# Tokens' values loaded behind the turn of P, with a fourth buffer of turned inputs, in a two-layer recurrent-memory attention kernel

## Chip, cores and metric

One core of one Trainium2 chip runs the whole program. The metric is the device time of one execution in microseconds, from runs without a profiler; the profile is one further execution with its own time.

## What is computed

Four sub-layers follow each other on x (2048 tokens, 512 features): attention with a recurrent memory (A), a dense layer with relu (B), A again, B again, each on the normalized input and added to x. A cuts the tokens into 64 segments of 32; each is preceded by 8 memory rows, which are the first 8 output rows of the segment before, so the segments of one A must run in order. 32 heads of 128. Cut from the reference:

```python
for s in range(n_seg):
    h = jnp.concatenate([mem, xs], axis=1)            # 8 + 32 rows
    q, k, v = (jnp.einsum('btd,dhe->bhte', h, W) for W in (Wq, Wk, Wv))
    scores = jnp.einsum('bhqe,bhke->bhqk', q, k) * scale
    p = softmax(jnp.where(mask, scores, -1e9))
    o = jnp.einsum('bhqk,bhke->bhqe', p, v)
    o = jnp.einsum('bhte,hed->btd', o, Wo)
    mem = o[:, :M, :]
    outs.append(o[:, M:, :])
...
x = x + A(layernorm(x)); x = x + relu(layernorm(x) @ w1) @ w2
x = x + A(layernorm(x)); x = x + relu(layernorm(x) @ w1) @ w2
```

## The kernel before

**Steps.** The program is written out as 68 steps, k = 0 to 67. Step k runs segment k of the first A (layer a = 0, k up to 63) and segment k - 4 of the second A (layer a = 1, k from 4), side by side: layer 0 on rows 0 to 39 of the tiles, layer 1 on rows 64 to 103. Steps 0 to 3 and 64 to 67 have one layer (`single`), steps 4 to 63 two. The dense layer of what ended two steps ago (`dense_h`, `dense_y`) and the output projection of the step before (`output_x`, tiles `wox`) run between as filler. TensorE, VectorE (DVE), SyncE (SP) and GpSimd (POOL) execute in the order in which the program is written; only ScalarE's (ACT) order is left to the scheduler.

**One two-layer step**, as `step` (L895) writes it: queries and keys of heads 0 to 15 (`qk`, L575); the value rows of this step's tokens are loaded from DRAM into `Vs` (`load_values`, called at L911); the normalized rows of earlier segments are turned by a DMA transpose (`transpose_step`, L289, tile `xnT`); the value rows of the memory are loaded (`load_memory_values`, L775); scores of these heads; then, behind the first batch of the queries of heads 16 to 31, `probabilities` (L926): softmax, whose last product into `P_sb` is POOL's (L646), and `turn_p` (L663), one DMA transpose of P into `PT0`, and in steps with k%4 = 3 `inputs_T`, a DMA transpose of 128 tokens of x. Dense and output filler; scores and softmax of the second half; `dense_y`; the second half of P is turned on TensorE (`transpose_p`, L656) and copied by ACT and DVE (L660); `weighted_v` (L682) multiplies P by `Vs`; `output_mem` (L617) and `new_memory` make the next memory: ACT copies `wm` (L814), TensorE turns it (`mt`, L820), and its values (`memory_values`, L765) are computed and stored to DRAM (L770).

**Values of tokens.** Layer 1's values are computed one step ahead (`values1`, L346) and stored to DRAM (`vd1`, L351). Layer 0's are, for k%4 < 2, a by-product of `memory_values` (DRAM tiles `vmd`); for the other two segments of each four they are computed in groups by `values0(p, n)` (L306): pair of segments p, and n of 0, 2, 4, 6, each 8 matmuls of 128x512, one ACT copy to a `vst` tile (L312) and one store to `vd0[p]` (L313). `load_values` therefore issues two DMAs (L742) for layer 0 and one (L737) for layer 1 when k%4 < 2, and one for each (L746, L737) otherwise. `values_at(k)` says which groups step k computes and `block` where they lie in it. In two-layer steps these are steps with k%4 = 1, where `output_x` has nothing to do. Before the change: step 1 three groups, step 5 two, steps 9 to 37 three each, steps 41 to 61 four each. `split(k)` (two or three groups) also splits `dense_h` around the second scores; with four groups it stays whole.

**Inputs.** x is handled 128 tokens at a time: `load_xb` (SP), `moments_x` (DVE, one `pow` on POOL), `normalize` (DVE, L227), `inputs_T` into `xT0[n]`. Step k handles n = k//4 + 3: load at k%4 = 0, moments at k%4 = 1, normalize at the end of k%4 = 2, transpose at k%4 = 3. `xT0` has three buffers; at step 1 a copy of n = 3 is turned on TensorE into the buffer of `ob`.

**SP's queue.** All DMAs but the loads of residual rows (POOL) and two at the end are issued by SP in program order; a DMA that waits for its data holds up all behind it.

Of the kernel before, what the change touches and what calls it, by code (L numbers as in the profile page):

```python
# [7 lines left out]
BF = mybir.dt.bfloat16  # L8
F32 = mybir.dt.float32
# [13 lines left out]
def kernel(  # L23
# [191 lines left out]
    xT0, xnT_tiles, hT_tiles, vd0, vd1, vmds, wm_tiles, wo_tiles, xp_tiles, vp_tiles, obs = {}, {}, {}, {}, {}, {}, {}, {}, {}, {}, {}  # L215

    def stat_tail(stats, of=""):
        mv = wk.tile([128, 2], F32, tag="ln_mv" + of, bufs=2 - len(of), name="mv")
        nc.vector.bn_aggr(out=mv[:], in_=stats[:])
        rstd = wk.tile([128, 1], F32, tag="ln_rstd" + of, bufs=2 - len(of), name="rstd")  # L220
        nc.vector.tensor_scalar_add(out=rstd[:], in0=mv[:, 1:2], scalar1=LN_EPS)
        nc.gpsimd.tensor_tensor(out=rstd[:], in0=rstd[:], in1=mhalf_t[:], op=ALU.pow)
        return mv, rstd

    def normalize(eng, dst, src, mom, lo, hi):
# [12 lines left out]
            nc.tensor.transpose(tp[:, c4, :], xn[:, c4 * 128:(c4 + 1) * 128], ident[:])  # L238
        return tp

    def inputs_T(n, early=False):
        tag, bufs = ("ob", 1) if early else ("xT0", 3)
        xT0[n] = wk.tile([128, NC4, 128], BF, tag=tag, bufs=bufs, name="xT0")
        if n < 3 or early:
            tp = transpose_pe(xbs[n])
            nc.scalar.copy(out=xT0[n][:], in_=tp[:])
        else:
            nc.sync.dma_start_transpose(out=xT0[n][:], in_=xbs[n][:])
# [47 lines left out]
    def values0(p, n, lo=0, hi=NC4, pool=None, stage=None):  # L296
        r = 64 * (p % 2)
        if (n, lo) == (0, 0):
            vd0[p] = dram.tile([4, 2, 64, 512], BF, tag="vd0", bufs=3, name="vd0")
        if lo == 0:  # L300
            pool, tag = (pool, "wo") if pool else (ps_fill, "fill")
            vp_tiles[p, n] = pool.tile([128, 512], F32, tag=tag, name="vp")
        vp = vp_tiles[p, n]
        for c4 in range(lo, hi):
            for j in range(2):
                nc.tensor.matmul(vp[64 * j:64 * j + 64, :], lhsT=xT0[p // 2][:, c4, r:r + 64],  # L306
                                 rhs=Wv_sb[:, c4, (n + j) * 512:(n + j + 1) * 512],
                                 start=(c4 == 0), stop=(c4 == NC4 - 1), tile_position=(0, 64 * j))
        if hi < NC4:
            return  # L310
        vst = wk.tile([128, 512], BF, tag="vst", bufs=5, name="vst")[:] if stage is None else stage
        nc.scalar.copy(out=vst, in_=vp[:])  # L312
        nc.sync.dma_start(out=vd0[p][n // 2].rearrange("j t e -> (j t) e"), in_=vst)  # L313
# [95 lines left out]
    def last_rows(k, eng):  # L409


        r = 64 * (LAST - k)
        R = residual(LAST - 1)
        if not last_t:
            last_t["stats"] = wk.tile([128, 2, 6], F32, tag="ln_last", bufs=1, name="stats")
            last_t["mv"] = wk.tile([128, 2], F32, tag="ln_mvl", bufs=1, name="mv")
            last_t["rstd"] = wk.tile([128, 1], F32, tag="ln_rstdl", bufs=1, name="rstd")
        stats, mv, rstd = (last_t[x][r:r + 64] for x in ("stats", "mv", "rstd"))
        nc.vector.bn_stats(out=stats[:, 0, :], in_=R[r:r + 64, 0:256])
        for j in range(2):  # L420
            nc.vector.tensor_copy(out=last_t["stats"][r + 32 * j:r + 32 * j + 32, 1, :],
                                  in_=last_t["stats"][r + 32 - 32 * j:r + 64 - 32 * j, 0, :])
        nc.vector.bn_aggr(out=mv, in_=stats.rearrange("p n s -> p (n s)"))
        nc.vector.tensor_scalar_add(out=rstd, in0=mv[:, 1:2], scalar1=LN_EPS)
        nc.gpsimd.tensor_tensor(out=rstd, in0=rstd, in1=mhalf_t[r:r + 64, :], op=ALU.pow)
        eng.tensor_scalar(out=XN[r:r + 64, 0:256], in0=R[r:r + 64, 0:256], scalar1=mv[:, 0:1], scalar2=rstd[:, 0:1],
                          op0=ALU.subtract, op1=ALU.mult)
# [234 lines left out]
    def turn_p():  # L662
        nc.sync.dma_start_transpose(out=PT0[:], in_=P_sb[:].rearrange("p s k -> p (s k)"))  # L663
# [116 lines left out]
    def block(k, lo, hi):  # L780
        output_x(k - 1, lo, hi)
        groups = values_at(k)
        if split(k):

            rest = [(i, 0, NC4) for i in range(1, len(groups))]
            if k == 1:
                todo = [] if lo == 0 else [(0, 0, 2)] if hi == 16 else [(0, 2, NC4)] + rest
            else:
                todo = [(0, 0, 2)] if lo == 0 else [(0, 2, NC4)] if hi == 16 else rest
        else:  # L790
            todo = [(i, c4, c4 + 2) for i in range(len(groups)) for c4 in range(0, NC4, 2)
                    if lo < 8 * i + 2 * c4 + 2 <= hi]
        for i, c_lo, c_hi in todo:
            p, n = groups[i]
            values0(p, n, c_lo, c_hi, ps_wo if i in (0, 3 if len(groups) == 4 else 2) else None)

    def split(k):
        return len(values_at(k)) in (2, 3)
# [1 line left out]
    def values_at(k):  # L800


        if k in (1, 5):
            return [(5, 6), (7, 0), (7, 2)] if k == 1 else [(7, 4), (7, 6)]
        if k % 4 != 1 or not has0(k + 1):
            return []
        groups = [(p, n) for p in range(9, NSEG // 2, 2) for n in range(0, NCH, 2)]
        i = k // 4 - 2
        lo = 3 * min(i, 8) + 4 * max(i - 8, 0)
        return groups[lo:lo + (3 if i < 8 else 4)]  # L810

    def new_memory(k, cont, wo):
        wm_sb = wm_tiles[k] = wk.tile([128, Dm], BF, tag="vst", bufs=5, name="wm")
        nc.scalar.copy(out=wm_sb[:], in_=wo[:])  # L814
        values1(k + 1, 0)
        c = 1 - k % 2
        mt = ps_c.tile([128, NC4, 2, M], F32, tag="c", name="mt")
        for c4 in range(NC4):
            for r in range(0, 128, 32):
                nc.tensor.matmul(mt[r:r + 32, c4].rearrange("p a m -> p (a m)"),  # L820
                                 lhsT=wm_sb[:, c4 * 128 + r:c4 * 128 + r + 32],
                                 rhs=sel[:, 4 * M * c:4 * M * c + 2 * M], start=True, stop=True,
                                 tile_position=(0, r))
        lo, hi = cont[0], cont[-1] + 1

        single = len(layers(k)) == 1
        by_act = k == 0 or has1(k + 1)

        def to_values():
            copy = nc.scalar.copy if by_act else nc.vector.tensor_copy  # L830
            copy(out=HTm[:, :, lo * M:hi * M], in_=mt[:, :, lo:hi, :].rearrange("p c a m -> p c (a m)"))

        def to_queries():
            nc.vector.tensor_copy(out=HT[:, :, lo:hi, 0:M], in_=mt[:, :, lo:hi, :])  # L834

        for f in (to_values, to_queries) if single else (to_queries, to_values):
            f()
# [57 lines left out]
    def step(k):  # L895
        act = layers(k)
        single = len(act) == 1
        cont = [a for a in act if k - DELTA * a + 1 < NSEG]
        n_x = k // 4 + 3
        has_x = n_x < NXT  # L900
        by_pe = k in (1, LAST)
        ahead = has1(k + 1) or not cont
        if k % 4 == 0 and has_x:
            load_xb(n_x)
        with tc.high_priority(offset=PRIO):
            behind = norm_rows.pop(k, None)
            if k == 1:
                def behind():
                    normalize(nc.vector, xbs[n_x], xbs[n_x], moments_x(n_x), 0, 128)
            qks = qk(0, act, behind=behind)  # L910
            load_values(k, act)  # L911
            if k == 1:
                memory_values(k)
                inputs_T(n_x, True)
        part = 4 if k == LAST else 8 if single else 5
        mid = 8 if k == LAST else 16

# [8 lines left out]
        def probabilities():  # L926

            softmax(0, act, by_pe, ess)
            if not by_pe:
                turn_p()  # L930
            if k % 4 == 3 and has_x:
                inputs_T(n_x)
            if has0(k + 1):
                load_x(k + 1)
            if k == 1:
                load_dense()
# [27 lines left out]
            add_output(k - 1)  # L964
        if k == LAST:
            add_last(k - 1, 0)
        if k % 4 == 1 and k > 1 and has_x:
            mom["x"] = moments_x(n_x)
        with tc.high_priority(offset=PRIO):
            transpose_p(1)  # L970
# [38 lines left out]
                memory_values(k + 1)  # L1009
        with tc.high_priority(offset=PRIO):  # L1010
            prepare(k + 1)
        if k % 4 == 2 and k > 2 and has_x:
            normalize(nc.vector, xbs[n_x], xbs[n_x], mom["x"], 0, 128)

    mom = {}
    with tc.manual_schedule(engines={mybir.EngineType.PE, mybir.EngineType.DVE, mybir.EngineType.SP,
                                   mybir.EngineType.Pool}):
        load_rest()
        mem0T = const.tile([128, NC4, M], BF)
        tp = transpose_pe(mem0)  # L1020
        nc.vector.tensor_copy(out=mem0T[:], in_=tp[:, :, 0:M])
        for a in range(2):
            nc.vector.tensor_copy(out=HT[:, :, a, 0:M], in_=mem0T[:])
            nc.vector.tensor_copy(out=HTm[:, :, a * M:(a + 1) * M], in_=mem0T[:])
        for n in range(2):
            m = moments_x(n)
            normalize(nc.vector, xbs[n], xbs[n], m, 0, 128)
# [74 lines left out]
```

## Time and profile before

| | us |
|---|---|
| three runs | 1595.73, 1600.38, 1601.42; median 1600.38 |
| the profiled execution | 1596.61 |
| its span, first to last instruction | 1594.8 |
| busy in it: PE / weight loads / DVE / ACT / POOL | 1565.9 / 1320.7 / 1268.4 / 738.9 / 349.8 |

The page names a group of instructions by line, engine, operation and tiles, with its count, busy time and mean duration. These are the groups that the change touches:

| group | count | busy us | mean ns |
|---|---|---|---|
| PE L306, value groups of layer 0 | 512 | 64.5 | 383 |
| PE L682, P times values | 4096 | - | 176 |
| ACT L312, copy of a group's values | 53 (+11 into weight tiles) | 30.6 | 582 |
| DVE L232, moments of x | 16 | 11.0 | 686 |
| DVE L227, normalize of x | 16 | 6.4 | 400 |

Matmuls overlap in the pipeline, so the mean duration of one says less than the time from the first of a run of them to the first of the next. An SP line shows only the issue of a DMA; when its data moves is seen in the trace's DMA packets, which carry a start, a size and a queue.

### The profile page before, as it was taken

To read this page: it belongs to the slowest core of one execution; us is meant where nothing else is said; L and a number is where in the kernel's file an instruction comes from. 1 tells how busy PE (TensorE), PEld (TensorE's weight loads), DVE (VectorE), ACT (ScalarE), POOL (GpSimd) and SP (SyncE) were. 2 spreads that over 40 slices of the span, in tenths; PEclk is the share of its full clock that TensorE was granted. 3 is DMA by queue.
4 is the path that set the end of the run, shared out by engine and by line. 5 is a ranking of instruction groups with operands and counts; after the bars stand their busy time and mean duration, and the time that the engine had idled before them with its cause. 6 is when DMAs were issued, how large, how long until landed. Compare 5 with 4: busy or idle time off the path is not lost.

```text
span 1594.8 us, 94682 instructions
## 1 busy us (share of the span) xinstructions
PE 1565.9 (98%) x42680; PEld 1320.7 (83%) x42680; DVE 1268.4 (80%) x3115; ACT 738.9 (46%) x1799; POOL 349.8 (22%) x670
## 2 busy tenths in 40 slices
PE   6999999999999999999999999999999999999998
PEld 4677888888898888889888888988888898898886
DVE  4578888888888888888888888888878888887866
ACT  3434444444544544454454545445454544545433
POOL 2012222222222222222222222222222222222110
PEclk9999999999999999999999999999999999999999
DMA  9733343343343534444334443343443333233332
GB/s 369 237 78 74 76 87 89 65 98 86 77 78 83 94 64 95 84 73 87 83 87 71 98 83 77 84 83 82 80 98 79 74 88 79 78 77 93 70 75 41
DMA packets 222564, 146.38 MB, mean 92 GB/s; under 512 B 124008, under 2 KB 216528, under 8 KB 222160
## 3 DMA queue, kind: packets, MB, share of 16 engines
q1 hardware_dynamic: 218992, 136.09, 37.6%
q8 instruction: 335, 5.49, 1.5%
q0 software_dynamic: 3072, 4.20, 1.1%
q14 instruction: 69, 0.57, 0.1%
q10 hardware_dynamic: 96, 0.03, 0.0%
HBM read 65.41 MB, written 45.35 MB: 69 GB/s over the span
## 4 chain that ended last, share of the span: by engine, by line
PE 96%; DMA 2%; DVE 1%; SPq 1%; issue 0%; ACT 0%; POOL 0%; POOLq 0%; ACTq 0%
PE qp L575 38%; PE wox L365 10%; PE wo L617 8%; PE vm L765 7%; PE v L346 7%; PE hp L507 6%; PE sp L528 5%; PE pv L682 4%; PE sp L609 4%; PE vp L306 3%; DMA Wv_sb<-in_A_Wv_dram 2%; PE tp L656 1%; PE xp L478 1%; PE wox L388 1%; SPq L134 0%; PE mt L820 0%
## 5 line engine op out<-in xcount | busy, mean ns | idle before, releaser
L581 ACT CAST QT<-qp 128x480 bf16<-128x480 f32 (+3 forms) x408 | 201.7, 494 | 392.3 <-PE qp L575 392.2
L575 PE MATMUL qp<-HT,Wq_sb 128*128 128x80 bf16 (+1 forms) x8704 | 370.2, 200 | 2.1 <-POOL HT L754 1.2
L575 PE MATMUL qp<-HT,Wk_sb 128*128 128x80 bf16 (+1 forms) x8704 | 369.2, 199 | 1.5 <-DMA Wk_sb<-in_A_Wk_dram 0.7
L575 PEld LDWEIGHTS <-Wq_sb 128*128 128x128 bf16 x8704 | 325.6, 100 | 33.8 <-issue 26.5
L575 PEld LDWEIGHTS <-Wk_sb 128*128 128x128 bf16 x8704 | 328.2, 100 | 2.3 <-DMA Wk_sb<-in_A_Wk_dram 1.2
L583 DVE CAST KT<-qp 128x480 bf16<-128x480 f32 (+3 forms) x408 | 231.4, 568 | 124.0 <-PE qp L575 118.1
L646 POOL TENSOR_TENSOR P_sb<-es,sm 128x320 bf16<-128x320 f32 x185 | 130.9, 721 | 751.7 <-ACT es L631 502.2
L365 PE MATMUL wox<-Wo_sb,OTx 128*64 128x256 bf16 x2880 | 173.6, 273 | 0.0
L625 DVE TENSOR_REDUCE mx<-sp 128x8 f32<-128x320 f32 x256 | 115.0, 487 | 73.6 <-PE sp L609 72.7
L365 PEld LDWEIGHTS <-OTx 128*64 128x64 bf16 x2880 | 150.2, 110 | 2.9
L631 ACT ACTIVATE es<-es 128x320 f32<-128x320 f32 x256 | 110.7, 469 | 58.2 <-DVE es L629 57.2
L765 PE MATMUL vm<-Wv_sb,HTm 128*32 128x512 bf16 x2176 | 136.4, 380 | 0.6 <-DVE HT L834 0.6
L641 DVE TENSOR_REDUCE sm<-es 128x8 f32<-128x320 f32 x256 | 118.3, 462 | 15.0 <-ACT es L631 4.7
L617 PE MATMUL wo<-Wo_sb,OTm 128*32 128x512 bf16 x2144 | 128.9, 380 | 0.2 <-issue 0.2
L346 PE MATMUL v<-Wv_sb,xnT 128*32 128x512 bf16 x2048 | 129.0, 378 | 0.0
L601 DVE CAST sp<-maskb 128x320 f32<-128x320 bf16 x256 | 118.4, 484 | 0.0
L629 DVE TENSOR_TENSOR es<-sp,mx 128x320 f32<-128x320 f32 x256 | 113.8, 483 | 1.5
L765 PEld LDWEIGHTS <-HTm 128*32 128x32 bf16 x2176 | 90.6, 96 | 27.4 <-issue 12.3
L528 PE MATMUL sp<-w_sb,hT 128*64 128x256 bf16 (+4 forms) x1452 | 104.1, 275 | 0.2 <-issue 0.2
L769 ACT CAST VmS<-vm 128x512 bf16<-128x512 f32 x134 | 78.6, 587 | 53.8 <-PE vm L765 53.8
L507 PE MATMUL hp<-xnT,w_sb 128*128 128x64 bf16 (+3 forms) x2948 | 102.2, 193 | 0.5 <-DVE xnT L436 0.4
L507 PEld LDWEIGHTS <-w_sb 128*128 128x128 bf16 (+1 forms) x2948 | 95.1, 101 | 1.3 <-issue 0.7
(124 smaller groups left out, 2028.8 us busy)
## 6 DMA issues: line engine op xcount, KB each, us to landing
Vs<-vd SPq DMA_DIRECT2D x96, 256.0 KB
vd<-vst SPq DMA_DIRECT2D x181, 128.0 KB
vmd<-VmS SPq DMA_DIRECT2D x134, 128.0 KB
Vs<-vmd SPq DMA_DIRECT2D x254, 32.0 KB
Vs<-vmd SPq DMA_DIRECT2D x60, 128.0 KB
Wq_sb<-in_A_Wq_dram SPq DMA_DIRECT2D x2, 2048.0 KB
Wk_sb<-in_A_Wk_dram SPq DMA_DIRECT2D x2, 2048.0 KB
Wv_sb<-in_A_Wv_dram SPq DMA_DIRECT2D x2, 2048.0 KB
```

The costliest lines, as they stand in the source:

```text
L346: nc.tensor.matmul(vp[32 * j:32 * j + 32, :], lhsT=tokens[:, c4, :], rhs=Wv_sb[:, c4, n * 512:(n + 1) * 512], start=(c4 == 0), stop=(c4 == ...
L365: nc.tensor.matmul(out[64 * j:64 * j + nr, 0:256], lhsT=lhsT, rhs=rhs[:, 256 * j:256 * j + 256], start=start, stop=stop, tile_position=(0, ...
L507: nc.tensor.matmul(hp[0:fs, fc - f0, 0:n], lhsT=w1_sb[:, c4, fc * 128:fc * 128 + fs], rhs=cols(c4), start=(c4 == 0), stop=(c4 == NC4 - 1))
L528: nc.tensor.matmul(sp_banks[bank][64 * j:64 * j + n, 0:w], lhsT=hT_tiles[d][0:fs, fc, 0:n], rhs=w2_flat[0:fs, fc * Dm + 256 * j:fc * Dm + ...
L575: nc.tensor.matmul(qp[:, hi, 0:ncol], lhsT=W_sb[:, c4, h * Dh:(h + 1) * Dh], rhs=HT[:, c4, a_lo:a_hi, :], start=(c4 == 0), stop=(c4 == NC4 ...
L581: nc.scalar.copy(out=dst[:, 0:nh, a_lo * L:a_hi * L], in_=qp[:, 0:nh, 0:ncol])
L583: nc.vector.tensor_copy(out=dst[:, 0:nh, a_lo * L:a_hi * L], in_=qp[:, 0:nh, 0:ncol])
L601: nc.vector.tensor_copy(out=sp_tiles[a], in_=maskb2)
L617: nc.tensor.matmul(wo[32 * j:32 * j + 32, :], lhsT=OTm[:, h, n, 2 * M * c:2 * M * c + 4 * M], rhs=Wo_sb[:, h, :], start=(h < 4), stop=(h > ...
L641: nc.vector.tensor_reduce(out=sm[:], in_=es[:], axis=AX.X, op=ALU.add)
L646: eng.tensor_tensor(out=P, in0=es[:], in1=sm[:].unsqueeze(2).to_broadcast([128, 8, L]), op=ALU.mult)
L765: nc.tensor.matmul(vp[32 * j:32 * j + 32, :], lhsT=HTm[:, c4, :], rhs=Wv_sb[:, c4, n * 512:(n + 1) * 512], start=(c4 == 0), stop=(c4 == NC ...
```

## The change

Three things are done. The groups of `values_at` are dealt out anew: (7, 4) goes to step 2, inside `new_memory`, between the copy of `wm` and the matmuls on it; (7, 6) to step 4, in the second part of `block`; the groups of pairs from 9 on begin at step 5 in place of step 9, three to a step up to step 49 and four in steps 53, 57 and 61. x is handled four steps earlier (n = k//4 + 4, beginning with a load, moments and normalize in step 2), `xT0` and `vd0` have four buffers, and the early copy in the buffer of `ob` is gone. In two-layer steps `load_values` is called in `probabilities`, behind `turn_p`, and no longer before `transpose_step`. Mean, variance and inverse deviation share a tile, the last rows' moments use a slot of `es`, and `mem0T` is gone: the turned memory is copied from PSUM four times.

```diff
     def stat_tail(stats, of=""):
-        mv = wk.tile([128, 2], F32, tag="ln_mv" + of, bufs=2 - len(of), name="mv")
-        nc.vector.bn_aggr(out=mv[:], in_=stats[:])
-        rstd = wk.tile([128, 1], F32, tag="ln_rstd" + of, bufs=2 - len(of), name="rstd")
+        mom = wk.tile([128, 3], F32, tag="ln_mv" + of, bufs=2 - len(of), name="mv")
+        mv, rstd = mom[:, 0:2], mom[:, 2:3]
+        nc.vector.bn_aggr(out=mv, in_=stats[:])
...
-    def inputs_T(n, early=False):
-        tag, bufs = ("ob", 1) if early else ("xT0", 3)
-        xT0[n] = wk.tile([128, NC4, 128], BF, tag=tag, bufs=bufs, name="xT0")
-        if n < 3 or early:
+    def inputs_T(n):
+        xT0[n] = wk.tile([128, NC4, 128], BF, tag="xT0", bufs=4, name="xT0")
+        if n < 4:
...
-            vd0[p] = dram.tile([4, 2, 64, 512], BF, tag="vd0", bufs=3, name="vd0")
+            vd0[p] = dram.tile([4, 2, 64, 512], BF, tag="vd0", bufs=4, name="vd0")
...
+        elif k < 5:
+            todo = [(0, 0, NC4)] if k == 4 and lo else []
...
     def values_at(k):
-        if k in (1, 5):
-            return [(5, 6), (7, 0), (7, 2)] if k == 1 else [(7, 4), (7, 6)]
+        if k < 5:
+            return {1: [(5, 6), (7, 0), (7, 2)], 2: [(7, 4)], 4: [(7, 6)]}.get(k, [])
...
-        i = k // 4 - 2
-        lo = 3 * min(i, 8) + 4 * max(i - 8, 0)
-        return groups[lo:lo + (3 if i < 8 else 4)]
+        i = k // 4 - 1
+        lo = 3 * min(i, 12) + 4 * max(i - 12, 0)
+        return groups[lo:lo + (3 if i < 12 else 4)]
...
         values1(k + 1, 0)
+        if k == 2:
+            values0(*values_at(k)[0])
         c = 1 - k % 2
...
-        n_x = k // 4 + 3
+        n_x = k // 4 + 4
...
-        if k % 4 == 0 and has_x:
+        if (k % 4 == 0 or k == 2) and has_x:
             load_xb(n_x)
...
             qks = qk(0, act, behind=behind)
-            load_values(k, act)
+            if single:
+                load_values(k, act)
...
             if not by_pe:
                 turn_p()
+            if not single:
+                load_values(k, act)
             if k % 4 == 3 and has_x:
                 inputs_T(n_x)
...
-        if k % 4 == 1 and k > 1 and has_x:
+        if (k % 4 == 1 and k > 1 or k == 2) and has_x:
             mom["x"] = moments_x(n_x)
...
-        if k % 4 == 2 and k > 2 and has_x:
+        if k % 4 == 2 and has_x:
             normalize(nc.vector, xbs[n_x], xbs[n_x], mom["x"], 0, 128)
...
-        mem0T = const.tile([128, NC4, M], BF)
         tp = transpose_pe(mem0)
-        nc.vector.tensor_copy(out=mem0T[:], in_=tp[:, :, 0:M])
         for a in range(2):
-            nc.vector.tensor_copy(out=HT[:, :, a, 0:M], in_=mem0T[:])
-            nc.vector.tensor_copy(out=HTm[:, :, a * M:(a + 1) * M], in_=mem0T[:])
+            nc.vector.tensor_copy(out=HT[:, :, a, 0:M], in_=tp[:, :, 0:M])
+            nc.vector.tensor_copy(out=HTm[:, :, a * M:(a + 1) * M], in_=tp[:, :, 0:M])
```

More of the change, by code (lines that the diff above doesn't have):

```diff
@@ L217, in stat_tail @@
     def stat_tail(stats, of=""):
-        mv = wk.tile([128, 2], F32, tag="ln_mv" + of, bufs=2 - len(of), name="mv")
-        nc.vector.bn_aggr(out=mv[:], in_=stats[:])
-        rstd = wk.tile([128, 1], F32, tag="ln_rstd" + of, bufs=2 - len(of), name="rstd")
-        nc.vector.tensor_scalar_add(out=rstd[:], in0=mv[:, 1:2], scalar1=LN_EPS)
-        nc.gpsimd.tensor_tensor(out=rstd[:], in0=rstd[:], in1=mhalf_t[:], op=ALU.pow)
+        mom = wk.tile([128, 3], F32, tag="ln_mv" + of, bufs=2 - len(of), name="mv")
+        mv, rstd = mom[:, 0:2], mom[:, 2:3]
+        nc.vector.bn_aggr(out=mv, in_=stats[:])
+        nc.vector.tensor_scalar_add(out=rstd, in0=mv[:, 1:2], scalar1=LN_EPS)
+        nc.gpsimd.tensor_tensor(out=rstd, in0=rstd, in1=mhalf_t[:], op=ALU.pow)
         return mv, rstd
@@ L414, in last_rows @@
         if not last_t:
-            last_t["stats"] = wk.tile([128, 2, 6], F32, tag="ln_last", bufs=1, name="stats")
-            last_t["mv"] = wk.tile([128, 2], F32, tag="ln_mvl", bufs=1, name="mv")
-            last_t["rstd"] = wk.tile([128, 1], F32, tag="ln_rstdl", bufs=1, name="rstd")
+            t = wk.tile([128, 8 * L], F32, tag="es", bufs=2, name="lm")
+            last_t["stats"] = t[:, 0:12].rearrange("p (n s) -> p n s", n=2)
+            last_t["mv"] = t[:, 12:14]
+            last_t["rstd"] = t[:, 14:15]
         stats, mv, rstd = (last_t[x][r:r + 64] for x in ("stats", "mv", "rstd"))
@@ L794, in block @@
             p, n = groups[i]
-            values0(p, n, c_lo, c_hi, ps_wo if i in (0, 3 if len(groups) == 4 else 2) else None)
+            values0(p, n, c_lo, c_hi, ps_wo if k % 4 == 1 and i in (0, 3 if len(groups) == 4 else 2) else None)
     def split(k):
@@ L908, in behind @@
                 def behind():
-                    normalize(nc.vector, xbs[n_x], xbs[n_x], moments_x(n_x), 0, 128)
+                    normalize(nc.vector, xbs[3], xbs[3], moments_x(3), 0, 128)
             qks = qk(0, act, behind=behind)
-            load_values(k, act)
+            if single:
+                load_values(k, act)
             if k == 1:
                 memory_values(k)
-                inputs_T(n_x, True)
+                inputs_T(3)
         part = 4 if k == LAST else 8 if single else 5
```

## The prediction

> **What bounds the kernel.** I read the chain of waits first, then cut the span into its 68 steps (a step starts at its first query matmul, every 128th `qp<-HT,Wq_sb` of the trace) and asked for the busy time of each engine in them.
>
> ```profile
> PE 96%; DMA 2%; DVE 1%; SPq 1%; issue 0%; ACT 0%; POOL 0%; POOLq 0%; ACTq 0%
> ```
>
> TensorE ends nearly everything, so only what TensorE does or waits for can count. Steps 2, 3, 4, 5, 9 and 41 (columns: window, length, busy time of PE, PEld, DVE, ACT, POOL with instruction counts, granted clock, DMA share, GB/s):
>
> ```profile
> 71.14:91.06 19.92, 17.98 (x551) 14.23 (x547) 11.66 (x32) 6.19 (x17) 2.21 (x6) 1.00 0.24 59
> 91.06:110.14 19.08, 18.95 (x582) 14.67 (x579) 14.49 (x37) 7.62 (x20) 3.72 (x8) 1.00 0.29 76
> 110.14:133.76 23.62, 22.54 (x711) 18.92 (x708) 20.19 (x52) 10.46 (x27) 4.74 (x9) 1.00 0.36 82
> 133.76:156.66 22.90, 22.07 (x596) 17.79 (x596) 19.14 (x47) 11.31 (x28) 5.05 (x10) 1.00 0.46 87
> 226.83:249.79 22.96, 22.95 (x605) 18.54 (x604) 19.15 (x47) 12.16 (x29) 5.66 (x11) 1.00 0.40 97
> 972.69:996.13 23.44, 23.44 (x612) 18.55 (x612) 19.14 (x47) 12.79 (x30) 5.66 (x11) 1.00 0.47 97
> ```
>
> Steps 2, 4 and 5 leave PE idle for 1.94, 1.08 and 0.83 us; step 9 (three value groups) and step 41 (four) leave it nothing, and step 41 is 0.48 us longer. The other steps repeat to 0.02 us (23.41, 23.39, 23.30 for k%4 = 0, 2, 3) although their DMAs do not land alike, so in steady state no DMA is on the path. Cutting all steps shows 6 us of PE idle time in steps 1 to 66 together, and five of the steps stray (13, 26, 27, 45, 52: 1.7 us in all).
>
> **The groups that leave late steps.** From the timeline of step 41:
>
> ```profile
> 984.84 3.19 PE L306 MATMUL vp<-Wv_sb,xT 128*64 128x512 bf16 x28
> 987.87 1.18 PE L528 MATMUL sp<-w_sb,hT 128*64 128x320 bf16 x18
> ```
>
> 28 matmuls fill 987.87 - 984.84 = 3.03 us, so 0.108 us each and 0.87 us for a group of 8. The fourth group costs a step only 0.48 of it (step 41 against 9), the rest fills small waits. The change takes it from steps 41, 45 and 49 (steps 53, 57, 61 keep four): 3 x 0.48 = **-1.45 us**.
>
> **Where the groups go.**
>
> ```profile
> 88.53 0.27 PE L820 MATMUL mt<-sel,wm 128*32 128x16 bf16 x16 [0.47 <-ACT wm L814]
> 126.21 0.48 PE L656 MATMUL tp<-ident,P_sb 128*64 128x80 bf16 x16 [0.94 <-POOL HT L754]
> 149.41 0.48 PE L656 MATMUL tp<-ident,P_sb 128*64 128x80 bf16 x16 [0.83 <-DVE P_sb L646]
> ```
>
> Each is a matmul (L820 of step 2, L656 of steps 4 and 5) that waits for another engine. Step 4: the group stands between the output matmuls and dense_y, ahead of a wait of 0.94 that is longer than 0.87: 0 (up to +0.1 for pipeline restarts). Its ACT copy (0.58, L312) falls where ACT idles 2.12 us before L660. Step 5: 0.87 into 0.83: +0.05. Step 2: the group lies in a wait of 0.47 for `wm`: 0.87 - 0.47 = +0.4; bounds 0.3 (the last dense_y matmuls are issued before their modelled end) and 0.87; I take 0.3, since they are issued every 0.06 us.
>
> **Work that comes earlier.** x is turned four steps sooner, so step 2 gets a load (0.40 on SP, while SP waits for the value load at 73.49 anyway), moments and a normalize on DVE. The moments (0.69 + 0.18 + 0.15, rows L232, L219, L221) stand between `P_sb` (ends 84.30) and the PT_sb copy at 85.10, which idled 0.81 before; in step 5 the same row of work takes 1.0 us from P_sb to copy, so the copy slips to 85.26: +0.16. The normalize (0.41, L227) stands at the start of step 3 ahead of the KT copy at 93.16; that ends at 93.57 and the third query batch starts at 93.62, for it reuses this PSUM buffer. PE would be there at 93.47, so +0.4 (bounds 0 and 0.45; I take 0.4). From step 4 on this work is where it was, on another tile. Ends: step 2 +0.46, step 3 +0.4, step 5 +0.05: **+0.9 us**.
>
> **Value loads behind the turn of P** (60 steps). SP in step 37 (from 879.62), and the reader:
>
> ```profile
> 880.87 0.89 SPq L742 DMA_DIRECT2D Vs<-vmd  x2
> 881.93 0.32 SPq L737 DMA_DIRECT2D Vs<-vd  x1
> 882.35 1.21 SPq L289 DMA_TRANSPOSE xnT<-XN  x1
> 883.60 2.59 SPq L775 DMA_DIRECT2D Vs<-vmd  x4
> 890.11 1.24 SPq L663 DMA_TRANSPOSE PT<-P_sb  x1
> 891.70 3.60 SPq L313 DMA_DIRECT2D vd<-vst  x3
> ```
> ```profile
> 895.99 0.49 PE L682 MATMUL pv<-PT,Vs 40*128 40x40 bf16 x25
> ```
>
> L742 and L737 move behind L663, which waits for POOL's P_sb until 10.5 us into the step, in every two-layer step. What they leave gains nothing: xnT may go 0.4 to 1.2 us sooner, but its first reader on PE is dense_h at 10.3. What is behind them is late by their 1.1 to 1.4 us of issue: the stores L313 (read a step or more later, one of five slots each) and for k%4 = 3 the turn of x (read steps later): 0.
>
> Do they land in time? In step 37 the last load is issued at 881.93 and the last of its 1024-byte packets start by 884.6: 2.65 us; in step 38, 904.59 to 907.25, 2.66. After the change, counted from the step's start: turn issued by 11.75; two loads (k%4 = 2, 3) put the last issue at 11.83 + 0.55 = 12.4, landing 15.0; three loads (k%4 = 0, 1) at 12.9, landing 15.5. The reader L682 starts at 16.78 (16.36 in steps of k%4 = 1 with three groups). So 1.7, 1.2 and **0.85 us** to spare.
>
> SP's issues stall now and then:
>
> ```profile
> L663 SPq DMA_TRANSPOSE PT<-P_sb x65: 1232/1244/2616, 79.3 to 1557.4; - x65
> L737 SPq DMA_DIRECT2D Vs<-vd x64: 302/318/1556, 113.8 to 1569.9; - x64
> L742 SPq DMA_DIRECT2D Vs<-vmd x60: 334/422/1641, 111.8 to 1442.7; - x60
> ```
>
> Minimum, median, maximum in ns: the turn ran over by about 1.1 us in 11 of 65, the value loads in some 17 of 156. Today nobody waits. Behind one another, a stall falls into this stretch in about 0.45 of the steps. Where three loads meet the early reader it costs 1.1 - 0.85 = 0.25 us: 15 x 0.45 x 0.25 = **+1.7 us** (bounds 0, and 5 where two stalls meet), elsewhere it is covered.
>
> **At nothing:** the moments in one tile (same engines, same waits); memory turned straight from PSUM (one copy of 0.17 less, four reads of PSUM instead of SBUF, 0.17 as L1021 to 0.22 as L834): TensorE waits until 37.71 for the second half of Wv, by the chain of waits; without this cover -0.2 to +0.2. last_rows in a slot of `es`: freed by a softmax of the last step long before. The fourth DRAM buffer has no instruction.
>
> **Sum.** -1.45 + 0.9 + 1.7 = +1.2 us on the profiled execution of 1596.61 (span 1594.8 and 1.8 around it): 1597.8. The median of the runs shown, 1600.38, is 3.8 above that execution, as two of three runs were; so I forecast 1600.4 + 1.2 = **1601.6**.
>
> **Rivals.**
> (a) *The loads land late*, in most two-layer steps: the slower side. If a load behind a transpose starts only once the turn has landed (13.2: its packets end at 915.75 in step 38, from 902.59) instead of at 11.75, the third lands at 13.2 + 1.06 + 2.65 = 16.9. Then k%4 = 1 pays 0.5 and 0 pays 0.1 each, and a stall of 1.1 us in 0.45 of all steps is paid nearly whole (0.8 where there are two loads): 15 x 0.6 + 30 x 0.45 x 1.1 + 30 x 0.45 x 0.8 = 35 us, 1635. It decides from a landing 0.85 us later than reckoned. For: L775, issued at 906.30 right behind a transpose, had its first packets only at 908.0. Against: those transposes had themselves waited behind the value loads until 906.75. Beside this stands a sentence of the Trainium skill ("DMA: Bandwidth & Descriptors", Latency and other measured facts): HBM access takes 0.2 us on average and 2 us under high load; as an estimate, 1.8 us more would put the third load at 17.3 and the time near 1623. The trace shows no such load: 2.65 us at a DMA share near 1.0.
> (b) *The fillers cost what they are*: 0.87 in each of steps 2, 4, 5 because copies or buffers of PSUM come in between: +1.8 more, 1603.4. Against: the waits named end on engines that the group does not use.
> (c) *All fits*: no stall shows, step 3 hides the normalize, and the strays go because early traffic is thinner: -1.45 + 0.5 - 1.7 = -2.7, 1597.7. Faster by over 8 us would need more than the idle time that there is, 6 us, and so a lucky set of runs.
>
> **Chances.** Forecast 0.62, (a) 0.14, (b) 0.10, (c) 0.14. A difference under 0.5% (8 us) can't be told from none here. Slower by more comes from (a): 0.14; faster by more from (c) with lucky runs: 0.04; the rest 0.82. Range 1594 to 1609: the spread of runs shown (1595.7 to 1601.4) with -2.7 to +5 on it, and (a)'s mild end.
>
> **What would show it.** PE gaps before L820 of step 2 and L656 of steps 4 and 5 gone; step 3 near 19.5; steps 41, 45, 49 at 22.96; L656 to L682 unchanged in two-layer steps, with Vs packets ending 15 to 15.6 us into them. I am wrong if L682 idles on a Vs DMA in more than a quarter of the steps, or if steady steps change length.

## The result, and the profile after

| | median us | runs | ratio to before (95% interval) |
|---|---|---|---|
| before | 1599.37 | 1595.73 to 1601.65 | |
| after | 1654.99 | 1644.62 to 1658.88 | 1.034 (1.0308 to 1.0372) |

The change costs 55.6 us, where 1.2 were forecast. The profiled execution took 1644.62 (span 1642.9, 48.1 longer than before). First the two lines of its chain of waits, by engine and by line:

```profile
PE 65%; DMA 15%; SPq 7%; issue 5%; POOL 3%; ACT 3%; DVE 1%; ACTq 0%; POOLq 0%
PE qp L575 27%; DMA Vs<-vd 12%; PE wo L617 8%; PE vm L765 7%; PE v L345 7%; SPq L663 4%; PE wox L364 3%; POOL P_sb L646 3%; PE pv L682 3%; ACT es L631 2%; PE sp L609 2%; PE vp L305 2%; PE hp L507 2%; DMA Wv_sb<-in_A_Wv_dram 1%; SPq L742 1%
```

TensorE ended 96% of the time before, now 65%. What replaced it is one path: P's product on POOL (L646), SP's issue of the turn (L663) and of the loads (L742), then the DMA into `Vs` (12% by itself). The view of waits (total us, times, mean us of one) names the reader:

```profile
PE pv L682 <- DMA Vs<-vd: 24.9, 41, 1.3
PEld L682 <- DMA Vs<-vd: 22.3, 36, 1.4
```

These are the matmuls and the weight loads of one instruction stream, so they overlap and are not added. Before, neither line existed. Step 37 on the timeline (it starts at 911.31; columns: start, duration, engine, line, operation, tiles, count, idle time before and its releaser):

```profile
921.79 1.25 SPq L663 DMA_TRANSPOSE PT<-P_sb  x1
...
923.09 1.56 SPq L742 DMA_DIRECT2D Vs<-vmd  x2
...
924.70 0.43 SPq L737 DMA_DIRECT2D Vs<-vd  x1
...
925.23 1.76 SPq L312 DMA_DIRECT2D vd<-vst  x3
...
928.40 0.18 PE L682 MATMUL pv<-PT,Vs 40*128 40x40 bf16 x1 [0.66 <-issue]
...
929.43 0.47 PE L682 MATMUL pv<-PT,Vs 40*128 40x40 bf16 x24 [0.85 <-DMA Vs<-vd]
```

The last load is issued at 924.70, 13.4 into the step (one of the two L742 took 1.10 us to issue, the other 0.41). One matmul of layer 0 goes at 928.40; the next, of layer 1, waits until 929.43. The trace's semaphore updates say when a DMA has landed: each of the 16 DMA engines raises the semaphore by one, and the reader waits for the last. For this load the last comes at 929.38, 0.05 ahead of the matmul.

Against the kernel `e3_behind_memory` below, which does the same work with the loads issued earlier, the 45.7 us of longer span divide like this. 44.2 lie in steps 6 to 63. Idle time of PE before L682 is 32.6 of them, in 48 of these 58 steps and in all four kinds of step. In three steps (23, 27 and 33) the granted clock fell to half for 3.413 us; these three are 5.2 longer than their idle time explains, 1.7 each. Some 6.4 are left, about 0.1 a step, which no view takes apart further. The small parts are read from these windows: steps 2, 3, 4, 5 and 41 of the changed kernel (columns as before: window, length, busy time of PE, PEld, DVE, ACT, POOL, clock, DMA share, GB/s):

```profile
70.91:90.86 19.95, 18.50 (x559) 14.41 (x555) 12.61 (x35) 6.86 (x18) 2.73 (x7) 1.00 0.29 79
90.86:110.80 19.94, 19.30 (x583) 14.80 (x579) 14.81 (x38) 7.59 (x20) 3.75 (x8) 1.00 0.28 72
110.80:135.35 24.55, 23.66 (x719) 19.20 (x715) 20.37 (x52) 11.02 (x28) 4.73 (x9) 1.00 0.33 79
135.35:159.10 23.75, 23.07 (x604) 18.33 (x604) 19.15 (x47) 11.87 (x29) 5.04 (x10) 1.00 0.39 94
1007.91:1032.06 24.15, 23.04 (x605) 18.57 (x604) 19.22 (x47) 12.11 (x29) 5.64 (x11) 1.00 0.39 89
```

Step 2 is as long as before with a group more. Step 3 has one layer, so no load moved in it, and is 0.86 longer. Steps 4, 5 and 41 now hold the wait at L682.

### The profile page after: what moved, and what is told of

Its sections match the earlier page's. It is cut to its first block, busy times and chain, and to the rows that moved or that the text cites. A ratio compares the mean times of both kernels' runs of the same rounds, so it can differ in the third digit from the quotient of the medians.

```text
span 1642.9 us, 94610 instructions
## 1 busy us (share of the span) xinstructions
PE 1579.2 (96%) x42680; PEld 1324.6 (81%) x42680; DVE 1270.7 (77%) x3114; ACT 737.4 (45%) x1799; POOL 349.2 (21%) x670
## 4 chain that ended last, share of the span: by engine, by line
PE 65%; DMA 15%; SPq 7%; issue 5%; POOL 3%; ACT 3%; DVE 1%; ACTq 0%; POOLq 0%
PE qp L575 27%; DMA Vs<-vd 12%; PE wo L617 8%; PE vm L765 7%; PE v L345 7%; SPq L663 4%; PE wox L364 3%; POOL P_sb L646 3%; PE pv L682 3%; ACT es L631 2%; PE sp L609 2%; PE vp L305 2%; PE hp L507 2%; DMA Wv_sb<-in_A_Wv_dram 1%; SPq L742 1%
## 5 line engine op out<-in xcount | busy, mean ns | idle before, releaser
L646 POOL TENSOR_TENSOR P_sb<-es,sm 128x320 bf16<-128x320 f32 x185 | 130.5, 719 | 749.2 <-ACT es L631 525.3
L617 PE MATMUL wo<-Wo_sb,OTm 128*32 128x512 bf16 x2144 | 132.3, 389 | 0.5
L682 PEld LDWEIGHTS <-Vs 40*128 40x128 bf16 x4096 | 64.6, 93 | 53.1 <-DMA Vs<-vd 22.3
L507 PE MATMUL hp<-xnT,w_sb 128*128 128x64 bf16 (+3 forms) x2948 | 103.0, 193 | 0.9 <-DVE xnT L436 0.4
```

What stands on the lines that cost most here:

```text
L507: nc.tensor.matmul(hp[0:fs, fc - f0, 0:n], lhsT=w1_sb[:, c4, fc * 128:fc * 128 + fs], rhs=cols(c4), start=(c4 == 0), stop=(c4 == NC4 - 1))
L617: nc.tensor.matmul(wo[32 * j:32 * j + 32, :], lhsT=OTm[:, h, n, 2 * M * c:2 * M * c + 4 * M], rhs=Wo_sb[:, h, :], start=(h < 4), stop=(h > ...
L646: eng.tensor_tensor(out=P, in0=es[:], in1=sm[:].unsqueeze(2).to_broadcast([128, 8, L]), op=ALU.mult)
```

## Experiments

Theory L (for late), formed on this: the loads are issued when the prediction said, but take 4.0 to 4.5 us to land instead of 2.65, so they come after their reader. Rivals: the loss is in the rest of the change (R); whatever stands behind the turn is held up by it (T); the loads hold each other up by their bytes (Q). All ratios are to the kernel before, run on the same chip (1597.78 in the first four experiments, 1598.11 in the next four, 1598.42 in the last).

### e1_move_alone: the kernel before, with only the value loads moved

```diff
-            load_values(k, act)
+            if single:
+                load_values(k, act)
...
                 turn_p()
+            if not single:
+                load_values(k, act)
```

> The kernel before with one edit: in two-layer steps the value loads are issued behind the turn of P. Theory T (the loads land after weighted_v wants them): 1648 to 1662 us, PE waiting on Vs in most two-layer steps, as in the changed kernel. Rival R (the earlier x, the dealt-out groups or the fourth buffers cost the time): 1597 to 1603 us.

Measured: 1647.63 (1645.41 to 1657.64), ratio 1.0323 (1.0291 to 1.0355). That is 0.4 below the range of T, and within the intervals the move alone makes the whole loss (ratio 1.0323, 1.034 for the changed kernel). 33.3 us of idle time stand before L682 in steps 6 to 63, and the half clock came six times.

### e2_rest_alone: the changed kernel, loads back at the head of the step

```diff
-            if single:
-                load_values(k, act)
+            load_values(k, act)
...
-            if not single:
-                load_values(k, act)
```

> The changed kernel with the value loads back at the head of the step. T: 1596 to 1602 us; by the terms of the prediction 0.5 us less than before, with step 2 0.46 longer, step 3 0.4 longer, step 5 0.05 longer and steps 41, 45 and 49 0.48 shorter each. R: 1645 to 1660 us.

Measured: 1598.88 (1598.07 to 1601.95), ratio 1.0007 (0.9998 to 1.0015). R falls. The 0.5 us that the terms of the prediction would have gained do not show. Without the late loads the small terms can be read; steps 2, 3, 4, 5 and 41 of this kernel:

```profile
71.29:91.08 19.79, 18.57 (x559) 14.46 (x555) 12.51 (x35) 6.86 (x18) 2.72 (x7) 1.00 0.29 75
91.08:110.95 19.87, 19.13 (x583) 14.73 (x579) 14.82 (x38) 7.59 (x20) 3.76 (x8) 1.00 0.29 73
110.95:135.06 24.11, 23.49 (x720) 19.10 (x716) 20.36 (x53) 11.02 (x28) 4.73 (x9) 1.00 0.39 85
135.06:157.96 22.90, 22.90 (x605) 18.26 (x604) 19.13 (x47) 11.87 (x29) 5.03 (x10) 1.00 0.41 92
974.38:997.37 22.99, 22.95 (x604) 18.53 (x603) 19.18 (x47) 12.10 (x29) 5.64 (x11) 1.00 0.41 94
```

Step 5 fills its 0.83 of idle time exactly (22.90 both times). Step 41 is 0.46 shorter than before (steps 45 and 49: 0.65 and 0.47), step 3 is 0.78 longer, step 4 0.49 longer, step 2 0.12 shorter.

### e3_behind_memory: the changed kernel, loads behind those of the memory values

```diff
             load_memory_values(k, act)
+            if not single:
+                load_values(k, act)
             scores(qks, act)
...
-            if not single:
-                load_values(k, act)
```

> The changed kernel with the value loads moved only behind the loads of the memory rows, ahead of the turn of P: issued about 5 us into the step, to land by 11, long before 16.4. T (lateness alone counts, not the place): within 2 us of the kernel with the loads at the head of the step. If the order behind the transpose of xnT itself did harm: 10 us or more above it.

Measured: 1597.41 (1595.7 to 1599.8), ratio 0.9998 (0.999 to 1.0007). Issued 3.4 us later than before the change (6.05 us into the step instead of 2.62), the last load takes as long as there (4.01 and 3.99 by the median), lands at 10.1, and no L682 waits. A later place costs nothing until the landing passes the reader.

### e4_busy_wait: the changed kernel, with PE kept busy ahead of L682

```diff
+        if not single:
+            keep_busy(4)
         with tc.high_priority(offset=PRIO):
             pvs = weighted_v(act)
```

> The changed kernel with four idle matmuls of 128x512 (0.86 us) in front of weighted_v in two-layer steps; they compute nothing that is used. They cost nothing where the wait for Vs is longer. If the half clock seen in the changed kernel's trace (0.50 for 3.4 us, three times) comes from PE idling in that wait, the mean granted clock is 1.000 and the runs agree within 6 us instead of 14; time 1645 to 1660. If the clock drops for another reason, it is 0.991 to 0.997 again.

Measured: 1684.62 (1678.02 to 1685.28), ratio 1.0531 (1.0513 to 1.0549). A miss, in the time and in the clock. The four extra matmuls stand in PE's order ahead of the wait, so they are paid in every step, and what lands after them is waited for all the same:

```profile
PE pv L682 <- DMA Vs<-vd: 16.9, 24, 1.1
```

The half clock still came three times, in steps of k%4 = 0 and 1 (20, 36 and 41), where a wait of 1.2 to 1.5 us was left. Steps of k%4 = 2 and 3 grew by 0.9 to 1.0 us over `e3_behind_memory`, nearly all of it filler, and wait hardly at all: there a reader 0.87 later (four matmuls of about 0.22) is late enough for most loads.

### e5_layer1_behind and e6_layer0_behind: one layer's loads moved

```diff
             if single:
                 load_values(k, act)
+            else:
+                load_values(k, [0])
...
-                load_values(k, act)
+                load_values(k, [1])
```

The diff is that of the first; in the second the layers are exchanged.

> Only layer 1's load (L737) stands behind the turn in two-layer steps; layer 0's loads are back at the head of the step. Theory L (a load takes 4.0 to 4.4 us from its issue to the last of its 16 semaphore updates, and only the last load's issue time counts): L737 is issued 0.5 to 0.9 us sooner than in the changed kernel, at 11.9 to 12.0 us into the step, and lands at 16.2 to 16.4 by the median, just ahead of a reader at 16.78 (16.36 in steps of k%4 = 1 with three groups). Only stalls of the issue and late sixteenth updates are paid: 1602 to 1618 us, no more than two half-clock windows. Rival T (whatever stands behind the turn is held up by the turn's own traffic until some 13.4): it lands near 17.2 as before, and the time is 1635 to 1655. Rival Q (the two loads hold each other up, through their 512 KB together): with one of them the time from issue to landing falls to 3 us or less, it lands by 15.2, and the time is 1597 to 1601.

> Only layer 0's loads (L742, two in steps of k%4 = 0 and 1; L746, one, in the others) stand behind the turn; layer 1's is back at the head. Theory L: the last issue is at 12.0 (one load) to 12.4 (two), from issue to last semaphore 3.4 to 4.0, so landings at 15.9 to 16.4: 1600 to 1614 us, a little under the kernel with layer 1's load alone. Rival T: 1630 to 1655. Rival Q: 1597 to 1601. The losses of this kernel and of the one with layer 1's load alone together stay well under the 50 us of both (theory L: it is a threshold, not a price for each load); if each load had its own price they would add up to about 50.

Measured: 1602.28 (1599.56 to 1605.51), ratio 1.0026 (1.0017 to 1.0035), and 1608.1 (1605.76 to 1613.74), ratio 1.0066 (1.0044 to 1.0088). Waits of the first, then of the second:

```profile
PEld L682 <- DMA Vs<-vd: 2.1, 8, 0.6
```
```profile
PE pv L682 <- DMA Vs<-vmd: 2.3, 2, 1.3
PEld L682 <- DMA Vs<-vmd: 2.2, 3, 1.3
```

Each half of the move costs 4 and 10 us, the whole of it 50 (`e1_move_alone`) to 56 (the changed kernel): a threshold, as L has it. Both times lie in their ranges. That layer 0's half would cost less than layer 1's was a miss, and layer 1's load landed a little sooner than expected.

T and Q fall as the whole cause: alone behind the turn, the load of layer 1 lands at 15.8 to 16.2 by the median of each kind of step, not near 17.2, and takes 3.95, not 3. In part both hold. The traces have this load in four settings (medians of 60, us from issue to last update):

| load of layer 1 (L737) | at the head of the step | behind the turn |
|---|---|---|
| with layer 0's loads just ahead of it | 3.99 (before) | 4.41 (after) |
| alone | 3.45 (`e6_layer0_behind`) | 3.95 (`e5_layer1_behind`) |

At the head some loads have updates missing from the trace; those with all 16 give 4.02 and 3.34. So the company of layer 0's loads costs it some 0.5 us, and the place behind the turn another 0.4 to 0.5 by the table. What it is in that place that slows the load, no run tells apart.

### e7_half_bytes: half the rows in each load

```diff
         for a in act:
+            n = SEG // 2 if k >= 8 else SEG
...
-                nc.sync.dma_start(out=Vs[64 * a + M:64 * a + L, :].rearrange("t (n e) -> t n e", n=NCH),
-                            in_=(vd1.pop(k) if a else vd0[0])[:].rearrange("i j t e -> t (i j) e"))
+                nc.sync.dma_start(out=Vs[64 * a + M:64 * a + M + n, :].rearrange("t (n e) -> t n e", n=NCH),
+                            in_=(vd1.pop(k) if a else vd0[0])[:, :, 0:n, :].rearrange("i j t e -> t (i j) e"))
```

The two loads of layer 0 are halved in the same way.

> The changed kernel, but from step 8 on each value load brings only half of its token rows (the other rows keep older values, so the values used are not the reference's): half the bytes and packets, the same number of loads at the same place. Theory L (most of the 4.4 us is a fixed time, from the issue to the first packet and from the last packet to the semaphore): landings come 0.3 to 0.6 us sooner, at 16.7 to 16.9, and 1612 to 1632 us. Rival Q (it is the bytes): issue to landing falls by 1.3 us or more, to 3 us, landings at 15.9, 1598 to 1606 us.

Measured: 1618.38 (1615.79 to 1620.79), ratio 1.0125 (1.0108 to 1.0143). With half the bytes the last load still takes 3.93 us (4.41 with all), lands at 16.5 to 17.0 by the median of each kind of step, and 15.7 us of idle time stand before L682 in steps 6 to 63. So 0.48 of the 4.41 goes with half the bytes; the rest does not.

### e8_later: two small stores ahead of the loads

```diff
             if not single:
+                for u in range(2):
+                    spare = dram.tile([1, 64], BF, tag="spare", bufs=4, name="spare")
+                    nc.sync.dma_start(out=spare[:], in_=ident[0:1, 0:64])
                 load_values(k, act)
```

> The changed kernel with two stores of 128 bytes on SP's queue between the turn and the value loads in two-layer steps, so that the loads are issued 0.6 to 0.7 us later. Theory L (nothing is left in hand, the reader waits for the landing in nearly every step): each of 60 steps is longer by that, 36 to 42 us, and a few more half-clock windows of 2 us: 1685 to 1705 us, L682 idle on Vs for 1.2 to 1.6 us a step. Rival (the steps are long for another reason, such as traffic that holds PE's weight loads or the copies up): 1650 to 1665.

Measured: 1680.04 (1671.67 to 1685.4), ratio 1.0506 (1.047 to 1.0542), a little under the expectation, and divided otherwise. The mean issue of the last load moved by 0.82 us (12.87 to 13.69), but it then took 4.13 instead of 4.51 by the mean, so it landed 0.44 later. The waits:

```profile
PEld L682 <- DMA Vs<-vd: 49.8, 64, 2.1
PE pv L682 <- DMA Vs<-vd: 43.1, 60, 1.9
```

Idle time before L682 in steps 6 to 63 rose from 32.6 to 53.7, and the half clock came eleven times there instead of three: 21 + 8 x 1.7 = 35 of the 38.2 by which the span is longer than the changed kernel's. Longer waits trip the clock far more often.

### e9_rest_trimmed: a try for the 1 to 2 us that the regrouping could bring

Loads at the head as in `e2_rest_alone`, and:

```diff
-            normalize(nc.vector, xbs[n_x], xbs[n_x], mom["x"], 0, 128)
+            normalize(nc.gpsimd if k == 2 else nc.vector, xbs[n_x], xbs[n_x], mom["x"], 0, 128)
...
-        if (k % 4 == 1 and k > 1 or k == 2) and has_x:
+        if k % 4 == 1 and k > 1 and has_x:
             mom["x"] = moments_x(n_x)
         with tc.high_priority(offset=PRIO):
             transpose_p(1)
+        if k == 2 and has_x:
+            mom["x"] = moments_x(n_x)
```

> The rest of the change with the loads at the head of the step, and its two costs in steps 2 and 3 taken away: the fourth x tile is normalized on POOL instead of DVE, and its moments stand behind the copies of the second turn of P instead of ahead of them. If the 0.78 us that step 3 had grown by comes from the normalize ahead of the KT copy, step 3 is back at 19.1, steps 41, 45 and 49 keep their 0.5 each, and the time is 1597.0 to 1598.2, ratio 0.9990 to 1.0000. If it has another cause (more DMA traffic in steps 2 and 3), step 3 stays at 19.9 and the time at 1598.9.

Measured: 1599.88 (1599.06 to 1603.02), ratio 1.0012 (1.0003 to 1.0021). A miss: step 3 is 0.31 longer than before instead of 0.78, but step 2 now 0.92 longer. The normalize was a cause in step 3, as expected; the two edits brought more than that into step 2, and which of them did is not told apart. No version tried beats the kernel before by more than its runs differ.

Landings in one table. Issue and landing of the last load of a two-layer step are medians in us from the step's start, steps 4 to 63; the reader, where it does not wait, starts at 16.78, in steps of k%4 = 1 with three groups at 16.36:

| kernel | issue | to last semaphore | landing | idle before L682 |
|---|---|---|---|---|
| before | 2.62 | 3.99 | 6.5 | 0 |
| `e3_behind_memory` | 6.05 | 4.01 | 10.1 | 0 |
| `e5_layer1_behind` | 11.83 | 3.95 | 15.8 to 16.2 | 1.7 |
| `e6_layer0_behind` (last load: layer 0's) | 11.8 to 12.5 | 3.73 | 16.0 to 16.4 | 5.1 |
| `e7_half_bytes` | 12.5 to 12.7 | 3.93 | 16.5 to 17.0 | 15.7 |
| after | 12.87 | 4.41 | 17.3 | 32.6 |
| `e8_later` | 13.2 to 13.8 | 4.12 | 17.3 to 17.9 | 53.7 |

The last column is a sum over steps 6 to 63; ranges are over the four kinds of step.

## Why the prediction was wrong, step by step

**The step that failed** is "In step 37 the last load is issued at 881.93 and the last of its 1024-byte packets start by 884.6: 2.65 us; in step 38, 904.59 to 907.25, 2.66." The packets are there, but the load has not landed with them. The same trace's semaphore updates tell it: for the load issued at 881.93 the last came at 886.78, 4.85 later and 2.2 after those packets; for the one issued at 904.59 at 908.37, 3.77 later and 1.1 after them. The forecast left this tail of 1.1 and 2.2 us out. The Trainium skill ("DMA: Bandwidth & Descriptors", Anatomy of one DMA) says, for DMAs of the other path, by GpSimd, that the update waits until the last byte is confirmed in the target memory and that this is most of the fixed cost of some 2.0 us. Over all 60 two-layer steps of the trace before, the time was 3.08 at the least, 3.99 by the median and 5.37 at most (in 16 of them some of the 16 updates are missing from the trace, and the last one recorded is taken): not one load landed in 2.65. With 3.99 as the term, the forecast's own sum puts the landings at 12.4 + 4.0 = 16.4 and 12.9 + 4.0 = 16.9: 0.4 to spare in half the steps and 0.1 to 0.5 too late in the other half. So the trace before could show most of the loss: its 60 times, put on the changed kernel's issue times, make the landings late by 27 us in all over steps 6 to 63, where the changed kernel's own times make it 40 (both counted against 16.78 and 16.36). The rest is the growth to 4.41 behind the turn, which only the runs showed. The packets are no safe sign there either: in the 44 steps of the changed kernel where the two layers' 512 packets were the only ones of 1024 bytes, the last packet ended 3.89 after the last load's issue by the median, not 2.65, and the last update came 0.50 after it.

**What held.** The issue times: forecast 12.4 for two loads and 12.9 for three, measured medians 12.48 and 12.87 to 12.97. The reader's start. That no DMA was on the path in steady state before, and that a move within the free time is free: `e3_behind_memory`. The stalls of the issue held in part: `e5_layer1_behind`, with 0.5 to 1.0 us in hand by the medians, waits 1.7 us in all before L682, the very number of the forecast, but only 0.8 of it in two steps with a late issue; 0.9 is in four steps where the load was issued in time and took 5.0 to 5.2. The agreement is chance.

**The regrouping.** Steps 41, 45 and 49: forecast -1.45, measured -0.46 - 0.65 - 0.47 = -1.58 in `e2_rest_alone` (step 45 was one of those that strayed before). Step 5: +0.05 forecast, 0.00. Step 2: +0.46 forecast, -0.12 and +0.55 in the two kernels with early loads. Step 3: +0.4 forecast, +0.78 and +1.26: the third query batch does wait 0.31 for the KT copy in both, near the 0.4, but matmuls of the dense layer (L507, which read `xnT`) wait another 0.30 and 0.40, which the forecast did not have and whose cause stays open. Step 4: 0 forecast, +0.49 and 0.00. In the timeline after, PE's wait of 0.94 before L656 of step 4, of 0.83 before that of step 5, and of 0.47 before the matmuls on `wm` in step 2 are gone, as said. Altogether a wash, as the forecast's -1.45 + 0.9 had it, but by errors that cancel: steps 2 to 4 missed by 0.4 to 0.6 each in `e2_rest_alone`, both ways. The start of step 2 moved from 71.14 to 70.91, and in the three kernels with early loads to 71.16, 71.29 and 71.45, so the edits put at nothing before it went a little past their bound of 0.2.

**Rival (a)** is what happened, with a chance of 0.14. Its own deciding point, a landing 0.85 us later than reckoned, was passed by far: 17.3 against 15.0 and 15.5. So was the sign that the forecast set itself, L682 idle on `Vs` in more than a quarter of the steps: it idled in 48 of 58. But the reason of (a) holds only in a small part. It let the loads start once the turn had landed. Their first packet moved at 13.06 by the median, 1.2 after the first issue, where the turn's last update came at 13.97; and the place behind the turn costs 0.4 to 0.5, not the 1.45 that (a) put on it. And 1635 was too little, for it kept the 2.65, and had no half clock in it. Of the sentence on HBM beside it (2 us more under load) no run here shows anything; the 2.65 that was set against it was the packets' time, not the landing's. Rivals (b) and (c) concern terms of 2 us and are settled by `e2_rest_alone`: steps 2, 4 and 5 grew by 0.4 together, not by 0.87 each as (b) had it, and step 3 does not hide the normalize as (c) had it.

## What to carry to other kernels

A DMA's landing is the last of its semaphore updates, not the bulk of its packets: take the time from issue to that update over all instances of the trace, with its spread, before a load is moved towards its reader. The price of a late load is a threshold: free until the landing passes the reader, then paid in nearly every step of a serial chain, here in 48 of 58. A load can also take longer at its new place, here by 0.4 to 0.5 us behind the turn, so a time read at the old place needs some slack. And a wait of TensorE beyond about 1.2 us may cost half the clock on top.

## What the runs showed of the hardware

**The sixteenth update can come late, with an instruction fetch in flight.** Instructions are fetched in packets of 16,384 bytes, about five a step, 0.9 to 2.0 us each (median 1.2). In the changed kernel such a packet lay wholly between issue and last update in 47 of the 60 loads of layer 1; there the last update came 0.35 us after the fifteenth by the median and 1.47 at most. In the 13 without one it was 0.02 and 0.31. In step 45 the turn had 15 updates by 13.80 and the last at 15.65, with a fetch packet from 13.10 to 14.44. That the fetch is the cause is argued, not shown: in the trace before, with the loads at the head of the step, the last update came at most 0.06 after the fifteenth, fetch or no fetch (44 loads with all 16 on record).

**The clock is decided on a fixed grid.** In each of the eleven traces all changes of the granted clock lie on a grid of 3.413 us (to 2 ns). Three neighbouring windows of it in step 27 of the changed kernel:

```profile
679.36:682.77 3.41, 2.18 (x87) 1.41 (x84) 1.88 (x7) 1.58 (x7) 0.00 (x0) 1.00 0.42 48
682.77:686.19 3.42, 3.42 (x36) 1.37 (x32) 1.57 (x4) 0.90 (x3) 1.22 (x2) 0.50 0.02 5
686.19:689.60 3.41, 3.41 (x80) 2.43 (x73) 2.83 (x7) 2.13 (x5) 0.07 (x1) 1.00 0.26 87
```

In the first PE is busy for 2.18 of 3.41 us (64%), with a wait of 1.05 for `Vs` in it; the next has half the clock and 36 matmuls instead of some 80; the third is whole again. By PE's busy share in a window, the next one was halved this often, over the windows of steps 0 to 63 in all traces together:

| PE busy in the window | windows | next one at half clock |
|---|---|---|
| under 0.50 | 4 | 4 |
| 0.50 to 0.60 | 17 | 13 |
| 0.60 to 0.65 | 15 | 6 |
| 0.65 to 0.70 | 15 | 2 |
| 0.70 and over | 4844 | 0 |

So a wait counts by how much of it falls into one window: that fits with waits of one length tripping the clock in some steps only, and with the spread of the changed kernel's runs: the mean clock was 0.997 in the fastest (1644.62) and 0.991 in the slowest (1658.88). The Trainium skill ("TensorE: Matmul & The Clock Gate", What's actually happening) has the free-running window of 3413 ns, and the traces agree. The rule of the same page's Part 1, half rate after an idle window of about 3.4 us, is too mild by these rows, where 1.2 us of idle time in one window were enough in 6 of 15 cases.
